# Opening the last feed-forward with weights already in SBUF, idle products in its layer norm, paired loads of the Wq and Wk tails, and a new product order

## The chip, the cores and the metric

One core of one Trainium2 chip runs the whole program. The metric is device time of one execution in microseconds (us), the median of several executions. TensorE (PE in the profile) multiplies matrices, VectorE (DVE), ScalarE (ACT) and GpSimd (POOL) do the element-wise work, SyncE (SP) issues most DMA transfers.

## The reference

Two layers, each a memory-augmented attention and a gated feed-forward with residuals. The attention walks over 64 segments of 32 tokens; eight memory rows go from each segment to the next, so it is a chain in time.

```python
x = A_x                                                # (1, 2048, 576)
for _ in range(2):
    x = x + _A_ref(_layernorm(x), mem0, Wq, Wk, Wv, Wo, 32)   # 32 heads of 128, 8 memory rows
    x = x + _B_ref(_layernorm(x), w1, w3, w2)                  # silu(x w1) * (x w3), then w2; 4608 wide

def _A_ref(x, mem0, Wq, Wk, Wv, Wo, seg_len):          # cut
    mem = mem0
    for s in range(n_seg):
        h = concat([mem, x[segment s]])                # 8 + 32 rows
        q, k, v = h @ Wq, h @ Wk, h @ Wv
        o = softmax(mask(q k^T / sqrt(128))) v @ Wo
        mem = o[:8]; outs.append(o[8:])
```

## The kernel before

Wq, Wk, Wv and Wo live in SBUF for the whole run. The feed-forward weights do not fit and are streamed, two ring slots at a time, for each job of 128 tokens. Both layers run interleaved, the second seven segments behind. A planner written in Python fixes the order of TensorE's work: one letter for each group of products (Q and q are the projections with 128-row and with 64-row contraction, S scores, T transposes, P probabilities times V, O and o the output projection, F, f and W the feed-forward, p the attention transposes, n the layer norm's transposes before a feed-forward).

```python
FIRST = ("maQQqQQqSq...")      # start up to the steady state, 813 groups
FOUR = ("QQqqQpQqqSVV...")     # four segments, 224 groups
LAST = ("QQpqqQQSqqVv...")     # the end, 654 groups
ORDER = FIRST + FOUR * 11 + LAST
```

The loads at the start: four full pieces of 128 rows and a tail of 64 rows for each of Wq and Wk. The tail of Wq goes to partitions 0 to 63, that of Wk to 64 to 127.

```python
def load_qk(self, kind):
    def f(n):
        wd = (self.a.wq, self.a.wk)[kind]
        for c in range(4):
            self.dma(self.T.W[:, 4 * kind + c, :], wd[c * P:(c + 1) * P, :])
        self.dma(self.T.W[kind * R64:(kind + 1) * R64, 8, :], wd[4 * P:D, :])
    return f
```

The last feed-forward has no attention beside it. Its nine weight blocks (two of the 18 column pairs each) are fetched over the attention weights once these have been read for the last time: blocks 0 to 2 over Wv, 3 to 7 over Wq and Wk, block 8 over Wo.

```python
if last:
    v_done, qk_done, o_done = last_reads
    tail = []
    for i in range(9):
        ...                                   # block 2 in two parts
        tail.append([load("tail", ..., em.tail_load(i, what), deps=dep) ...])
for pp in range(NPR // 2):                    # blocks in order 0 to 8
    for pr_ in (2 * pp, 2 * pp + 1):
        if last:
            w13 = w2 = None
            ld = tail[pp]
        else:
            w13, w2 = Slot("w13"), Slot("w2", users=ne)     # ring slots
            ...
```

## Time and profile before

| | before |
|---|---|
| time | 2783.58 us median, three runs, 2782.71 to 2785.88 |
| span of the profiled execution | 2782.7 us |
| TensorE busy / weight loads busy | 2725.4 / 2245.9 us (98% / 81%) |
| VectorE / ScalarE / GpSimd busy | 2041.0 / 1093.0 / 328.4 us |
| DMA | 323.80 MB, mean 116 GB/s |
| mean granted TensorE clock | 0.993 |

The prediction shows the lines that matter. Two ways of reading are needed for them. In a window, TensorE's busy time near the window's length means that only less work on TensorE, or work at a higher clock, would help there. In a timeline, the bracket at a line's end is TensorE's idle time before that line and what ended it; "issue" stands there when no semaphore explains the idleness.

### The profile page before, as it was taken

How to read it: one execution, taken by the hardware profiler on the slowest of the kernel's cores; microseconds unless marked ns; L12 is line 12 of the kernel's file. 1: busy time of each engine (PE TensorE's matmuls, PEld its weight loads, DVE VectorE, ACT ScalarE, POOL GpSimd, SP SyncE). 2: the span in 40 equal slices, each digit the busy share in tenths (PEclk: the TensorE clock that was granted, in tenths of full speed). 3: DMA queues.
4: the chain of work that ended last, by engine and by line, in shares of the span. 5: the costliest groups of instructions: out<-in, count | busy, mean ns of one | idle time of the engine just before them, and what ended most of it. 6: DMA issues, size and time to landing. Idle time of an engine off the chain costs nothing.

```text
span 2782.7 us, 136378 instructions
## 1 busy us (share of the span) xinstructions
PE 2725.4 (98%) x60909; PEld 2245.9 (81%) x60909; DVE 2041.0 (73%) x5559; ACT 1093.0 (39%) x3364; POOL 328.4 (12%) x399
## 2 busy tenths in 40 slices
PE   5999999999999999999999999999999999999998
PEld 3888878888888888888888888888888888888886
DVE  4677777777777777777777777777777777677765
ACT  1434443433434344343434434343443434343332
POOL 1111010110101011010101101010110101011110
PEclk9999999999999999999999999999999999999998
DMA  8072614234241423424142342414244241423468
GB/s 307 4 207 67 178 56 139 82 111 132 74 139 49 147 82 112 131 75 137 52 145 82 114 130 74 139 52 143 82 116 128 77 139 56 132 84 114 143 180 244
DMA packets 483436, 323.80 MB, mean 116 GB/s; under 512 B 26296, under 2 KB 478400, under 8 KB 481184
## 3 DMA queue, kind: packets, MB, share of 16 engines
q1 hardware_dynamic: 479824, 308.15, 37.5%
q8 instruction: 476, 7.80, 1.1%
q0 software_dynamic: 3024, 6.93, 0.8%
q14 instruction: 112, 0.92, 0.1%
HBM read 310.26 MB, written 2.36 MB: 112 GB/s over the span
## 4 chain that ended last, share of the span: by engine, by line
PE 96%; DMA 1%; DVE 1%; issue 1%; ACT 1%; POOL 0%; SPq 0%; DVEq 0%; ACTq 0%; POOLq 0%
PE bank L538 83%; PE YB L538 13%; DMA W<-in_A_Wk_dram 1%; DMA WO<-in_B_w_dram 0%; DVE STAT L544 0%; ACT OT L541 0%; DVE PB L544 0%; DMA W<-in_A_Wq_dram 0%; DVE SME L544 0%; ACT HT L541 0%; ACT SME L541 0%; DVE XR L544 0%; ACT PTS L541 0%; DVE PTS L544 0%; ACT QKT L541 0%
## 5 line engine op out<-in xcount | busy, mean ns | idle before, releaser
L538 PEld LDWEIGHTS <-W 128*128 128x128 bf16 (+1 forms) x29040 | 1228.7, 98 | 147.9 <-issue 44.2
L538 PE MATMUL bank<-HT,W 128*128 128x80 bf16 (+3 forms) x22720 | 817.7, 198 | 20.6 <-DMA W<-in_A_Wk_dram 12.6
L538 PE MATMUL bank<-XTB,W 128*128 128x256 bf16 (+3 forms) x6320 | 657.5, 262 | 0.3 <-DMA W<-in_B_w_dram 0.3
L895 POOL MEMSET PB<- 128x1024 bf16 x284 | 270.2, 951 | 2134.4 <-PE bank L538 1529.1
L541 ACT ACTIVATE QKT<-bank 128x64 bf16<-128x64 f32 (+1 forms) x1382 | 320.2, 314 | 448.6 <-PE bank L538 441.2
L538 PE MATMUL YB<-OT,WO 128*128 128x80 bf16 (+3 forms) x11360 | 431.5, 199 | 4.8 <-ACT OT L541 3.9
L538 PEld LDWEIGHTS <-WO 128*128 128x128 bf16 (+1 forms) x11400 | 388.5, 102 | 44.6 <-issue 26.9
L538 PE MATMUL bank<-WV,HT 128*32 128x512 bf16 (+1 forms) x6840 | 381.1, 383 | 0.8 <-issue 0.8
L544 DVE CAST QKT<-bank 128x256 bf16<-128x256 f32 (+2 forms) x682 | 184.1, 317 | 186.9 <-PE bank L538 185.5
L538 PE MATMUL bank<-W2C,HTT 128*128 128x288 bf16 x2232 | 312.9, 287 | 0.0
L544 DVE TENSOR_REDUCE STAT<-SME 104x8 f32<-104x320 f32 (+1 forms) x568 | 270.9, 477 | 56.4 <-ACT SME L541 53.5
L538 PEld LDWEIGHTS <-HT 128*32 128x32 bf16 (+1 forms) x6840 | 150.3, 95 | 180.0 <-issue 56.3
L544 DVE TENSOR_TENSOR PB<-SME,STAT 40x128 bf16<-40x128 f32 (+1 forms) x1004 | 283.9, 321 | 12.6 <-DVE STAT L544 0.9
L541 ACT ACTIVATE HTT<-bank 128x512 bf16<-128x512 f32 (+1 forms) x324 | 176.4, 550 | 261.8 <-PE bank L538 261.4
L538 PEld LDWEIGHTS <-HTT 128*128 128x128 bf16 x2304 | 209.9, 98 | 54.3 <-issue 1.5
L544 DVE SCALAR_TENSOR_TENSOR XR<-bank,XR 128x288 f32<-128x288 f32 x576 | 239.5, 448 | 12.3 <-PE bank L538 7.4
L541 ACT ACTIVATE SME<-SME 104x320 f32<-104x320 f32 (+1 forms) x284 | 133.5, 470 | 265.7 <-DVE SME L544 265.1
L544 DVE SCALAR_TENSOR_TENSOR HTT<-HTT,bank 128x512 bf16<-128x512 bf16 (+1 forms) x324 | 201.8, 623 | 41.6 <-ACT HTT L541 38.9
L541 ACT ACTIVATE OT<-bank 128x320 bf16<-128x320 f32 (+1 forms) x352 | 138.1, 413 | 214.7 <-PE bank L538 214.6
L544 DVE TENSOR_TENSOR HTT<-HTT,bank 128x512 bf16<-128x512 bf16 (+1 forms) x324 | 203.5, 628 | 22.4
L544 DVE TENSOR_TENSOR SME<-bank,maskb 104x320 f32<-104x320 f32 (+1 forms) x284 | 135.7, 484 | 113.2 <-PE bank L538 106.7
L541 ACT ACTIVATE V<-bank 128x512 bf16<-128x512 f32 x248 | 138.4, 596 | 181.6 <-PE bank L538 181.2
(64 smaller groups left out, 1707.7 us busy)
## 6 DMA issues: line engine op xcount, KB each, us to landing
W<-in_B_w_dram SPq DMA_DIRECT2D x612, 256.0 KB, 3.5
W2C<-in_B_w_dram SPq DMA_DIRECT2D x306, 288.0 KB, 3.2
W<-in_B_w_dram SPq DMA_DIRECT2D x612, 32.0 KB, 3.1
W<-in_B_w_dram SPq DMA_DIRECT2D x10, 512.0 KB, 8.3
WO<-in_A_Wo_dram SPq DMA_DIRECT2D x4, 1152.0 KB, 16.6
XR<-in_A_x_dram POOLq DMA_DIRECT2D x16, 288.0 KB, 3.7
W<-in_A_Wq_dram SPq DMA_DIRECT2D x4, 1024.0 KB, 8.3
W<-in_A_Wk_dram SPq DMA_DIRECT2D x4, 1024.0 KB, 17.3
```

The lines of the kernel that those rows point to most:

```text
L538: self.ch("PE", self.nc.tensor.matmul(out, lhsT=lhsT, rhs=rhs, start=start, stop=stop, skip_group_check=True, **k))
L541: self.ch("ACT", self.nc.scalar.activation(*a, **k))
L544: self.ch("DVE", getattr(self.nc.vector, fn_)(*a, **k))
L895: return lambda n: self.ch("POOL", self.nc.gpsimd.memset(self.T.PB[:, pb.i], 0.0))
```

## The change

It has four parts. The last feed-forward begins with block 8, whose weights its predecessor left in the two ring slots, so eight blocks are fetched. Ten products of the identity with 512 columns of Wo, whose result nobody reads, stand before the transposes of the last layer norm to keep TensorE's clock up. The two 64-row tails are issued one after the other, behind all full rows. And the three order strings are new throughout; in the last one the predecessor's down-projection (W) moves ahead of the layer norm's transposes (n).

```diff
+        npp = NPR // 2
+        for at, pp in enumerate([npp - 1] + list(range(npp - 1)) if last else range(npp)):
+            stays = last and pp == npp - 1
             for pr_ in (2 * pp, 2 * pp + 1):
-                if last:
+                if stays:
+                    w13, w2 = kept[pr_]
+                    ld = []
+                    w2s.append(w2)
+                elif last:
                     w13 = w2 = None
                     ld = tail[pp]
                 else:
-                    w13, w2 = Slot("w13"), Slot("w2", users=ne)
+                    keep = s0 < nst <= s0 + 4 and pp == npp - 1
+                    w13, w2 = Slot("w13", users=1 + keep), Slot("w2", users=ne + keep)
+                    kept[pr_] = w13, w2
 ...
-            for i in range(9):
+            for i in range(8):
 ...
     def f(n):                                   # load_qk
-            self.dma(self.T.W[kind * R64:(kind + 1) * R64, 8, :], wd[4 * P:D, :])
+            if kind:
+                for r, wd in ((0, self.a.wq), (1, self.a.wk)):
+                    self.dma(self.T.W[r * R64:(r + 1) * R64, 8, :], wd[4 * P:D, :])
 ...
     def f(n):                                   # ln_tr
+            for _ in range(10 if warm else 0):
+                self.mm(self.T.YB[:], self.T.ident[:], self.T.WO[:, 0, 0:512], True, True)
             for c in range(5):
                 ...                             # the transposes
 ...
-    "maQQqQQqSq..."   ... "pnWFFffFfFWfFfFW..."  # FIRST, FOUR, LAST rewritten
+    "maQQqqSQQq..."   ... "pWnFFffFfFWfFFffW..."
```

More of the change, by code (lines that the diff above doesn't have):

```diff
@@ L187 @@
 FIRST = (
-    "maQQqQQqSqQqqSQqQQqqSSTVvVPTPvTOoPOToXOPxoOoQQqqQQSqqQqSQqVQqvSTQqPTSOPOToPoTOPoOoaQQqqVSvQQqqQQqqSTVSPvQqQqTOSP"
-    "oXTOPoTOPoOoxQQqqQQSqqQqSQVvqQSTqQqPSOoTPTOPoTOPoOoQQpqqQQqqSVSvQnQqqFTFffVSPvQTQqPqOFfOTFoSoPfWOXxTFfPFOoofWQQq"
-    "qQQSqqFQfqSFWQfqVvSTQqPFTQfPqOSWoFTOPfoFTOfPWOooFQQqqfaQFfqSWQQqFfVvQSqqWTFFffVPvSWQQqqOSTFfPFfToOWoPTPOOoobQQqq"
-    "QQSqqXQxSqQTQqVvqSPQTqOPSXxToOPoTOPoOoQQpqqQQSqqVVSvvQnTQqqQPqSQTFfqFOfPSoTOFoPfXxOTFPfWOooFQfqFQqfQWQSqqVvSQWQq"
-    "qQTFqfSPQTFqfXxSFOofPWOTFfPoTaFfPOOWooFQqfQQqqFQqfVSvWQFqfQFSqWQSfqQTFfqVSvWPFfTFfPOToWPOoTOPobOoXxQpqQQqqXxSQQq"
@@ L193 @@
-    "qVSTvQqPQqSTQqOPSoTOPoOTPonOoQQqqQpQqqSVVvvQTQqSqPQQSqqnOTFfPFoSfXxTFfPOWWFTOofPFOfooWFWQqfQQqqFQqfXxSWWQQqqVSvT"
-    "FQfqFQPfqSTOWWaFoSPfFTOofPWTOPFWOFooffVvWQQqqQqSQWFfqQQTqqSWFfPSQOTWqFfPFQqfVSoWWFTfvOPoTWPOOoobQQpqqVQSqvQQqQqS"
-    "qQSqXTxQqPTSXxPOoTOPoTWPOOoon"
+    "maQQqqSQQqQQqSQqqTqSQVvVqPvTOPSToOPXOToPoxOoQQqqQQSqqQSqVQqvQSTqPQTqPSTOoPOOToPoaOoQQqqQQqqSVSvQQqqQTSqQqPVSTOPv"
+    "oTXPOToPOOooxQQqqQQSqqQqSQQqVSqQqvTSPTOPoTOPoTOPoOoQQpqqVQvqSQnQqqFQqfSTFfPSQQqqWFTOPfSoFOfVvTWFPfoXTFPOOoofxQqQ"
@@ new lines @@
+    "QqqQFSqfVSvQWQqqQTqSQPqFfOTFfPSoTWPOFofOTFPfoOoWQQqqFQfqVvWFQqfSFQSfqVvWQFqfQSqTFfPQOTqWFPfSoTFPfOOWToPoOoabQQqq"
+    "QQqqSVSvQQqqXxTSXxPQTQqqOSPToPOOToPoOoQQpqqQQSqqQQqqSVVvvTnQPqSFTQPfqOFSofXTOoPxWTFFfPfOOooWQQqqFfQFSfqQQqqVSvQT"
+    "QqqFQPfSqFWSfXTFfPxOTOWooPFTFffPOOooWQFqfQqQFafqQWFSqfQQqqSFWQqfVVSvvFfTQqPWFSfTFfPOToWPOoTOPoOboQQqqQpQSqqQXxSQ"
+    "qqVSvQqTQPqXTSPxOTOoPoTPOOoonQQpqqQQSqqVnQqSvQQqqFTfFPfQOTqSoFWVvSfPFTWOPfXTOFxofPFOWooWQfqQQqqQFfqSVvWFWQTqfSQX"
+    "xqFWQqPfSWQTOqPFoSfOTFPfoWFTWOPfFOooWQfqQQqQqqSWQFfqSVvFTQqWQqfWaQqPFSSfTFVvfPOWWFTfoOPoTWPOOoobQQqqQQSqqQQSqqVX"
@@ L196 @@
+    "TvSxQqPQTqOoSPXxTOPopTWPOOoon"
 )
 FOUR = (
-    "QQqqQpQqqSVVvvQTQqPqSnQQSqqOFTFPffoSXxTOWWFPfoTFPfOOFooWQqfQFfqQWQSqqXVxvQTQqqWWFSSfPFQfqOFTQqfFPfoSWWOTFPfoTOFf"
-    "PWOooWQQqqFQqfSWQWQqqFQSfqVvTFWQqPfSWFQfqTOFfPoSWWFVvfTOPoTWPOOooabWQQqqQQSqqQQqqVSSvXxTQqPQqTOPSXxoTOPopTOPoOon"
+    "QQqqQpQSqqVVvvQTQqqPSnQFQSqqfOTFPfSoXxTFfPFWWOFToffPOOooWWFQfqQQqqQFqfSFWWQfqXVxvSQTWQqqFPfSTWQFPfqOOToSoWFPfFTO"
+    "PfWOooFQfqQQqqWWFQqfVSSvQQqqWFTQqfPSWFQfqVvSTWWFFPffOoTOPoTWPOoOoabWQQqqQQSqqQQqqVSSvXxTQqPQqTOPSXxoTOPopTOPoOon"
@@ L200 @@
 )
 LAST = (
-    "QQpqqQQSqqVvnQFfqQSqQTqFPfFTOSPQqfVOWvoSoTFPWOTfXxoPFOfoWFWQqfQQqqFQSqfXVxvWWQTFqfSFQqfQqQqPSFTWOWPfSoTOPFWOToof"
-    "PFOfoWQQqqVvFQfqSWWFQfqFQqfQqSWTFPfQQSqqWTFSPfVvWTWOFfoOPoTWPOoOobQQqqQpQSqqQQqqSXVxSvQqTQPqTXxPSOOoTWPToPOOoonQ"
-    "QpqqVSvQqQQnqqQTFPSqfQQSqqOFTfVvPFToSfPOWOooWTFPfXOWxoWQQqqVSvFQqfQqFQQqqfSTFPfQSqWWOFTQqfFPfoSTWWFOPfoTFPfWWOOF"
-    "oofFQqQfqQqSWQWFqfFfTQQSqqQWqWFQqfSVvFfPSWOWTFfPVovTWPTOoPOOoobWQQQqqqpQSVXqxvQSnQqqFfTQSPqQFqfOFToSfPWTOFPfoTOP"
-    "FOfooWQQqqQFqfSQFqfVSvQQqqQTWFqfPSQTqFOoSfPVvFTOPWTOoofPFOoXfxQWQqqVSvQFfqQFqfQSqWTQFfqQSqQPqFTSOfPoWTOPFTofPOOo"
@@ L207 @@
-    "oFQqQqfQQSqqWQSqVvQTQQqqqSPSTVPvFOOTooPfTOoPOopnWFFffFfFWfFfFWfFfFfWFfFfWFfFWfFfFWfFFffWFfFfWW"
+    "QQqqQpQqqSVvSQnQqqQTqQFqPfSSFTOPfVvFTOoofPFWWTOPfoFOfoWQWFqfQQqqWFWQSfqVXxvQSqXxQqTFQqPfSQFfqOTFWPfoSWOTFfPFTOoo"
+    "fPWOWoFQqfFWWQqfFQSfqQVvqQWQSqqWTFQfqQSPqWFTOSoPfVWFvfTOPoTWPOOoobQqpQQqqQSqQqSXVvxQTqQSPqQTqXPSOxoOTWPToPOOoonQ"
+    "QqqpQSqVQnvqQTSqPFQfqFQTOqfPSFQOqfVoSovWWTFfPFTOPfWOFWooXxQqfVQqvQQSqqWQqSFTQqfFWQQqSqPfTFSPfOWTOooWPFTFfPfOOooW"
+    "WQFfqQqFQQqfqSWFWQqfSVvFQfqWWSFQqfTFfPQqWTWOFSoPfVvTOWoPTWPOObooQQpqqQQSqqQQqqSnXVvxFfSTQqPQFTqfOoSPFTOoPfWTOPFO"
@@ L208 @@
+    "fooFQqfQqVSQvQqqWQTFfqFSPfVQqvWTQFSfqFQPqfOOoSoWTFfPXxTFPfWOOooFQfqQqQQSqqQSVqvWQTFfqQSPqFfQqTOSoPWOTFPfoTFfPOOo"
+    "oWQqFQfqQQSqqVvSQQqqQTQqqSPTSVPFvOToOPoTfOoPOopWnFFffFfFWfFFffWFfWFfFfFWfFfFWfFFffWFfFfWFfFfWW"
 )
@@ L260, in make_nodes, with ln_nodes @@
     steps = [{} for _ in range(nst)]
-    def ln_nodes(tag, src, xn, deps, prio, writes):
+    def ln_nodes(tag, src, xn, deps, prio, writes, warm=False):
         a = node("DVE", 1.16, em.ln_stats(src, xn), deps=deps, prio=prio, acq=[] if src is xn else [xn], name=tag + "stats")
@@ L267, in ln_nodes @@
         b = Slot("bank", users=len(writes))
-        d = node("PE", 5 * 0.056, em.ln_tr(xn, b), deps=[c], prio=prio, mode="full", acq=[b], rel=[xn], name=tag + "tr")
+        d = node("PE", 5 * 0.056, em.ln_tr(xn, b, warm), deps=[c], prio=prio, mode="full", acq=[b], rel=[xn], name=tag + "tr")
         out = []
@@ L385, in step @@
             last_reads[1].extend(me[f"QKt{u}"] for u in range(8))
-            last_reads[2].extend(wots[:2])
         nxt = [li for li in ls if t - LAG * li + 1 < nseg]
@@ L408, in make_nodes @@
     last_up = [None]
-    last_reads = [], [], []
+    last_reads = [], []
+    kept = {}
     def job(j):
@@ L425, in job @@
             pa = post(bi, g)
-            wr += ln_nodes("F", xr[g], Slot("xn"), [pa], s0, [((lambda bi: lambda b: em.xtb_write(bi, b))(bi), cost, [prev_ff])])
+            wr += ln_nodes("F", xr[g], Slot("xn"), [pa], s0, [((lambda bi: lambda b: em.xtb_write(bi, b))(bi), cost, [prev_ff])], last)
         mm = (128 * ne / 2.4 + 2.5) / 1000
@@ L430, in job @@
         if last:
-            v_done, qk_done, o_done = last_reads
+            v_done, qk_done = last_reads
             tail = []
-            for i in range(9):
+            for i in range(8):
                 if i == 2:
@@ L436, in job @@
                 else:
-                    parts = [(None, 9 * 512 + 4 * 576, v_done if i < 2 else qk_done if i < 8 else o_done)]
+                    parts = [(None, 9 * 512 + 4 * 576, v_done if i < 2 else qk_done)]
                 tail.append([load("tail", kb(128, c), s0 + o.tail_at + 0.01 * i, em.tail_load(i, what), deps=dep) for what, c, dep in parts])
-        for pp in range(NPR // 2):
+        npp = NPR // 2
+        for at, pp in enumerate([npp - 1] + list(range(npp - 1)) if last else range(npp)):
             mids, w2s, htts, lds = [], [], [], []
+            stays = last and pp == npp - 1
             for pr_ in (2 * pp, 2 * pp + 1):
-                prio = s0 + o.ff + (o.win if s0 + 4 < nst else o.last_win) * pr_ / NPR
-                if last:
+                prio = s0 + o.ff + (o.win if s0 + 4 < nst else o.last_win) * (2 * at + pr_ % 2) / NPR
+                if stays:
[3 more added lines that the diff above has]
+                elif last:
                     w13 = w2 = None
@@ L453, in job @@
                 rel13 = [w13] if w13 else []
-                fm = node("PE", 16 * mm, em.ffn_up(ents, pr_, w13, b, last, False), deps=wr + ld, prio=prio, mode="full",
+                fm = node("PE", 16 * mm, em.ffn_up(ents, pr_, w13, b, last and not stays, False), deps=wr + ld, prio=prio, mode="full",
                           acq=b + [htt], name="FF")
-                ff = node("PE", 2 * mm, em.ffn_up(ents, pr_, w13, b, last, True), deps=[fm], prio=prio + o.fft, mode="row",
+                ff = node("PE", 2 * mm, em.ffn_up(ents, pr_, w13, b, last and not stays, True), deps=[fm], prio=prio + o.fft, mode="row",
                           rel=rel13, name="FFt")
@@ L464, in job @@
                 b = banks()
-                d = node("PE", 8 * 0.1225, em.ffn_down(bi, pp, htts, w2s, b, last), deps=mids + lds, prio=prio + o.w2,
+                d = node("PE", 8 * 0.1225, em.ffn_down(bi, pp, htts, w2s, b, last and not stays), deps=mids + lds, prio=prio + o.w2,
                          mode="full", acq=b, rel=htts + w2s, name="W2")
@@ L638, in f @@
             T = self.T
-            qk, wv, wo = T.W[:].rearrange("p a b -> p (a b)"), T.WV[:], T.WO[:].rearrange("p a b -> p (a b)")
+            qk, wv = T.W[:].rearrange("p a b -> p (a b)"), T.WV[:]
             n13, n2 = 9 * 512, 4 * D
@@ L645, in f @@
                 t13, t2 = wv[:, 2 * k:2 * k + n13], qk[:, 5 * k:5 * k + n2]
-            elif i < 8:
+            else:
                 t13, t2 = qk[:, (i - 3) * k:(i - 3) * k + n13], qk[:, (i - 3) * k + n13:(i - 2) * k]
-            else:
-                t13, t2 = wo[:, 0:n13], wo[:, n13:k]
             fa = i * 512
@@ L714, in lnps, with ln_tr @@
         return self.bk_bf(b, 5 * P).rearrange("p (c t) -> p c t", c=5)
-    def ln_tr(self, xn, b):
+    def ln_tr(self, xn, b, warm=False):
         def f(n):
+            for _ in range(10 if warm else 0):
+                self.mm(self.T.YB[:], self.T.ident[:], self.T.WO[:, 0, 0:512], True, True)
             for c in range(5):
```

## The prediction

> **What bounds the kernel now.** I read the page first, then the windows (busy time per stretch), then the chain of waits at both ends, then TensorE's timeline. The windows say where time can be had. Columns: stretch, length, then busy microseconds and instruction counts of TensorE, its weight loads, VectorE, ScalarE and GpSimd, then TensorE's granted clock, DMA share, GB/s.
>
> ```profile
> 20.00:40.00 20.00, 10.53 (x328) 9.68 (x329) 5.64 (x16) 2.72 (x9) 0.00 (x0) 1.00 1.01 376
> ...
> 1000.00:1500.00 500.00, 499.23 (x10804) 411.85 (x10797) 376.49 (x1025) 201.35 (x613) 58.63 (x70) 1.00 0.36 105
> ...
> 2720.00:2740.00 20.00, 13.57 (x393) 11.08 (x390) 12.41 (x34) 5.69 (x21) 4.36 (x5) 0.80 0.88 269
> 2740.00:2760.00 20.00, 20.00 (x248) 16.33 (x248) 11.26 (x29) 5.12 (x12) 0.58 (x1) 0.85 1.10 332
> 2760.00:2783.00 23.00, 16.51 (x201) 12.36 (x198) 11.74 (x29) 3.64 (x9) 0.00 (x0) 0.93 0.62 188
> ```
>
> Between about 66 and 2720 us TensorE is full: 499.23 of 500 us in the middle, at full clock, DMA at a third. Nothing but less TensorE time helps there. The first 60 and the last 50 us are different: DMA saturated, TensorE partly idle and partly at half clock. All three named edits are at those ends. The chain that ended last, in order of time (start, length, what):
>
> ```profile
> 1.62 5.19 DMA W<-in_A_Wq_dram
> 6.81 0.02 issue
> 6.83 21.51 DMA W<-in_A_Wk_dram
> 28.34 0.05 issue
> ...
> 2739.88 23.16 PE bank L538 x289
> 2763.04 9.57 DMA WO<-in_B_w_dram
> 2772.61 0.05 issue
> 2772.66 5.90 PE bank L538 x50
> ```
>
> The start waits for Wk until 28.34. The end waits for the ninth weight block, which lands at 2772.61, and then does the last block's products, 5.90 us. The timeline of that end (start, length, work, count, idle before and its releaser):
>
> ```profile
> 2769.32 1.15 PE L538 MATMUL bank<-W,HTT 128*128 128x288 bf16 x8
> 2770.91 0.40 PE L538 MATMUL bank<-XTB,WO 128*128 128x128 bf16 x4 [0.44 <-DMA WO<-in_B_w_dram]
> 2772.66 3.52 PE L538 MATMUL bank<-XTB,WO 128*128 128x128 bf16 x36 [1.35 <-DMA WO<-in_B_w_dram]
> ```
>
> **What the Trainium skill says.** "TensorE: Matmul & The Clock Gate", Part 1: after about 3.4 us of idleness the clock halves, and it returns only after a busy window of that length; windows run free of the kernel. The trace agrees: the 2 us windows show clock 0.50 from 2734 to 2744 and 1.00 from 2746, and again 0.50 in 2774 to 2776 after the DMA wait. "SBUF — State Buffer", Door 1, says a 64-partition transfer reaches half of the DMA ports; agreed: while the Wq tail (64 rows of 8192 bytes, 0.52 MB) was in turn, 14 to 16 us moved 217 GB/s, against 397 just before and 418 from 18 us on. The same page, "Can I just issue two DMAs to hit both halves?", says no: two such DMAs gained 6% over one. If so, loading the tails together saves no transfer time. "Runtime: NRT & Kernel Launch", Instruction fetch mechanics: each sequencer fetches its instructions in 16 KiB blocks by DMA. That fits idle time that the trace puts to "issue" only while DMA is saturated (3.44 us before 43.87, 2.04 us before 2733.22); that the fetch causes it is my inference.
>
> **The change part by part.**
>
> *Last feed-forward.* Before: nine weight blocks of (9 x 512 + 4 x 576) x 128 x 2 bytes = 1.77 MB are fetched, issued from 2722.25, landed at 2772.61: 15.9 MB in 50.4 us, 316 GB/s. After: eight, because block 8 is still in the two ring slots where the previous feed-forward left it. The last weight lands about 1.77 MB / 0.33 MB per us = 5.4 us sooner, near 2767.2. In the changed order as many products follow the last read of Wq/Wk as before, so the transfers start equally early.
>
> TensorE's own need: one block in steady state takes 2756.44 - 2753.01 = 3.43 us on the timeline (40 products of 128 columns, 8 of 288). Nine take 30.9 us. Blocks started at 2742.30, so unhindered they would end at 2773.2; they ended at 2778.5. The missing 5.3 us: DMA waits of 0.26 + 0.44 + 1.35 = 2.05; half clock from 2742.30 to about 2745.8, half of 3.5 = 1.75; half clock for about 3.4 us of the last block, about 1.7. The sum, 5.5, closes the account. With block 8 first, block 7 is last, needed at 2742.3 + 8 x 3.43 = 2769.7 and landed at 2767.2: 2.5 us of margin, so the waits (2.05) and the cold last block (1.7) go. At full clock the last product waits for tanh and two multiplications (0.38 + 0.42 + 0.42, against 0.98 us of other products): 0.5 comes back. Gain: 3.2.
>
> *Idle products.* Ten of 512 columns stand in the order after the attention transposes and the predecessor's last down-projection (8 of 288), before the layer norm's transposes. They can run once the attention output has been read, 2735.7. If the clock is down, as before: transposes 0.5, down-projection 1.9, ten at 512/1.2 GHz = 4.3 (0.43 each is an estimate from that skill page), so they end at 2742.5 unless a full busy window ends sooner; the normalised rows are ready at 2739.88. They then delay the transposes by 1 to 2.6 us. In return the down-projection no longer stands between transposes and feed-forward (it had put the start to 2742.30, where the 0.70 us write of the transposed rows alone would allow about 2741.4), and the feed-forward runs warm: +1.75. Net about 1. If the clock never drops: 0.3 + 1.0 + 2.2 = 3.5, ending by 2739.3, no delay, start 2741.3: gain 1.0 + 1.75 = 2.75. Before, it dropped at 2732.2 after the 2 us issue gap, which the same saturated DMA makes likely again, so I weigh the cold case at 60%: gain 1.7.
>
> *Start.* In 14 to 18 and 26 to 30 us, against 422 GB/s, (205 + 107 + 189 + 156) x 2 us = 1.31 MB were not moved: 3.1 us lost to two half-width tails. Wv's two tails already lie side by side; the same count from 38 to 46 us (312, 252, 317, 390) gives 0.83 MB, 2.0 us. So I expect some 1 us saved in transfers. Wk's full rows also come 2.5 us sooner, but TensorE then only reaches Wv sooner, whose full rows come with the transfers. I keep 1.5.
>
> *Product order.* It is rewritten for the whole program, with the same number of groups of each kind. What it can change is switches of array tiling, and waits. One switch costs 0.1 us:
>
> ```profile
> 1004.74 1.15 PE L538 MATMUL bank<-W2C,HTT 128*128 128x288 bf16 x8
> 1005.82 0.46 PE L538 MATMUL bank<-PTS,V 64*128 64x80 bf16 x16
> ...
> 1009.59 1.14 PE L538 MATMUL bank<-W2C,HTT 128*128 128x288 bf16 x8
> 1010.57 5.25 PE L538 MATMUL bank<-HT,W 128*128 128x80 bf16 x144
> ```
>
> The same eight products take 1.08 us up to a group in another tiling, 0.98 up to one in the same. Counting neighbours in the order strings: first part 515 switches before, 508 after; the part repeated eleven times 114 and 114; last part 383 and 375. That is 15 fewer, 1.5 us. The repeated part carries two thirds of the time and ends in the same 40-odd groups, so I give it 0 with an error of 0.3 us a turn, 3 us in all: a new wait there counts eleven times.
>
> *Sum.* 3.2 + 1.7 + 1.5 + 1.5 = 7.9 us of 2783.58: 2775.7.
>
> **The rivals.**
> *The order decides.* Eleven turns multiply any new wait: 0.5 us a turn costs 5.5 us and the total is 2781; 0.3 us better gives 2772. For it: the order strings differ nearly everywhere. Against: the middle already idles only 0.77 us in 500, so there is little to win, and equal switch counts speak for equal time.
> *Idle products in the way.* If they run cold to the end and the layer norm waits, the feed-forward starts at 2743.9, and its clock gain is eaten: 2777.5. For: granted clock 0.50 through 2734 to 2744. Against: they themselves fill the window.
> *DMA stays the bound.* If saturated transfers run slower or start later, the margin of 2.5 us goes, TensorE waits for block 7 and cools again: about 2779. Against: DMA share stays at 1.10 there, and 1.77 MB less must move.
> *Tails don't overlap.* Then the start gains nothing in transfers and the total is about 2777.
>
> **Range and chances.** The parts are small and mostly independent: errors of about 2 at the end, 1.5 at the start, 3.5 from the order make some 4.5 together. So 2775.7, with 2768.5 to 2782. Two per cent is 56 us, more than the start's and end's idle time that this could remove, and no part can cost that: within 2% is nearly sure.
>
> **What would show it.** Right: no DMA wait of TensorE after the last layer norm, granted clock 1.00 for nearly all of the last feed-forward, about 31 us from its first product to its last; the Wk wait of the chain ends some 2 to 3 us sooner; a turn of the repeated part as long as before (162.2 us from one turn's first product to the next's in the trace), with TensorE over 99.5% busy. Wrong: new idle time before TensorE in the middle, transposes held back past the normalised rows by more than 2.6 us, or a DMA wait of TensorE for the eighth block.

## The result and the profile after

The changed kernel took 2775.48 us median (2774.15 to 2775.73, four runs); the kernel before in the same session 2783.59 us (2782.71 to 2785.88). The ratio is 0.9969, with a 95% interval of 0.9951 to 0.9986. Ratios here are the mean time of one kernel's fast runs over the mean of the other's in the same rounds, so they are not quite the ratio of the medians. The predicted time was 2775.7 us.

Windows of the changed kernel, in the columns that the prediction explains:

```profile
20.00:40.00 20.00, 11.10 (x304) 9.97 (x305) 5.90 (x17) 2.61 (x10) 0.32 (x1) 0.94 1.01 346
1000.00:1500.00 500.00, 499.23 (x10828) 415.20 (x10825) 374.82 (x1023) 201.87 (x611) 58.27 (x70) 1.00 0.36 105
...
2730.00:2750.00 20.00, 18.92 (x228) 14.16 (x228) 11.76 (x31) 4.23 (x10) 1.13 (x2) 0.91 1.10 331
2750.00:2772.00 22.00, 17.55 (x234) 13.60 (x232) 13.47 (x33) 4.41 (x11) 0.00 (x0) 0.99 0.70 210
```

The middle is as full as before, to the last digit: 499.23 of 500 us. The end is fuller and mostly at full clock. The chain that ended last, start and end of it (start, length, what):

```profile
2.02 7.37 DMA W<-in_A_Wq_dram
9.40 20.50 DMA W<-in_A_Wk_dram
...
2754.70 9.08 DMA W<-in_B_w_dram
2763.79 0.05 issue
2763.83 2.32 PE bank L547 x36
```

The wait for Wk did not end sooner: 29.90 against 28.34 us before. It is now the Wk tail that ends it, not the full rows. At the end a transfer still stands in the chain, but it is the eighth block's and it lands at 2763.79, not the ninth's at 2772.61. The timeline of that end shows what the wait is worth:

```profile
2762.67 0.39 PE L547 MATMUL bank<-XTB,W 128*128 128x128 bf16 x4
2763.83 2.28 PE L547 MATMUL bank<-XTB,W 128*128 128x128 bf16 x36 [0.77 <-DMA W<-in_B_w_dram]
2766.04 2.43 PE L547 MATMUL bank<-W,HTT 128*128 128x288 bf16 x16
```

There is one wait of 0.77 us where there were three of 2.05 us together, and the 36 products of the last block take 2.28 us against 3.52 before: they run at full clock.

**Where the time went between the two profiled executions** (spans 2782.7 and 2772.4 us; the changed kernel's profile is of its fastest run, so the whole difference is 10.3 us here and 8.1 us in the medians). The milestones are first products of groups, in each trace; the rows sum to 10.1 us, and the other 0.2 lie after the last product:

| stretch | before | after | difference |
|---|---|---|---|
| start to the first product of the repeated part | 552.95 | 549.88 | -3.1 |
| eleven turns of the repeated part | 1784.11 (162.2 each) | 1784.46 (162.2 each) | +0.4 |
| from there to the first transfer of the last weights | 385.19 | 384.47 | -0.7 |
| from that transfer to the attention's transposes | 13.53 | 11.45 | -2.1 |
| from these to the first product of the last feed-forward | 6.52 | 6.34 | -0.2 |
| from that to the last product | 36.25 | 31.87 | -4.4 |

The largest part is the last feed-forward, as predicted. Two entries need an explanation: 3.1 us at the start though all of Wk came no sooner, and 2.1 us before the attention's transposes, where the change did nothing. The second is an idle time put to issue that the kernel before has and this execution has not. It is the last of these lines of the kernel before's timeline:

```profile
2730.92 0.27 PE L538 MATMUL bank<-PTS,V 64*128 64x40 bf16 x7
2733.22 0.21 PE L538 MATMUL bank<-PTS,V 64*128 64x40 bf16 x1 [2.04 <-issue]
```

These are eight products of one group, with the same semaphores behind them, and 2.04 us between the seventh and the eighth.

### The profile page after: what moved, and what is told of

It is laid out like the page before. It is cut to its first block, busy times and chain, and to the rows that moved or that the text cites. A ratio compares the mean times of both kernels' runs of the same rounds, so it can differ in the third digit from the quotient of the medians.

```text
span 2772.4 us, 136269 instructions
## 1 busy us (share of the span) xinstructions
PE 2723.5 (98%) x60919; PEld 2252.7 (81%) x60919; DVE 2047.1 (74%) x5584; ACT 1091.0 (39%) x3339; POOL 328.4 (12%) x399
## 3 DMA queue, kind: packets, MB, share of 16 engines
HBM read 308.49 MB, written 2.36 MB: 112 GB/s over the span
## 4 chain that ended last, share of the span: by engine, by line
PE 96%; DMA 2%; ACT 1%; DVE 1%; issue 0%; SPq 0%; ACTq 0%; DVEq 0%
PE bank L547 82%; PE YB L547 14%; DMA W<-in_A_Wk_dram 1%; DMA W<-in_B_w_dram 1%; DMA WV<-in_B_w_dram 0%; SPq L556 0%; DMA W<-in_A_Wq_dram 0%; ACT OT L550 0%; DVE STAT L553 0%; ACT HT L550 0%; DVE SME L553 0%; ACT PTS L550 0%; DVE PB L553 0%; DVE PTS L553 0%; ACT QKT L550 0%
## 5 line engine op out<-in xcount | busy, mean ns | idle before, releaser
L547 PE MATMUL bank<-XTB,W 128*128 128x256 bf16 (+1 forms) x6360 | 658.2, 261 | 1.6 <-ACT XTB L550 0.8
L550 ACT ACTIVATE QKT<-bank 128x64 bf16<-128x64 f32 (+1 forms) x1348 | 312.6, 315 | 445.0 <-PE bank L547 434.4
L553 DVE CAST QKT<-bank 128x64 bf16<-128x64 f32 (+1 forms) x716 | 193.6, 316 | 243.5 <-PE bank L547 242.3
L550 ACT ACTIVATE PTS<-bank 128x320 bf16<-128x320 f32 (+1 forms) x386 | 146.5, 411 | 206.1 <-PE bank L547 143.0
L550 ACT ACTIVATE V<-bank 128x512 bf16<-128x512 f32 x269 | 147.2, 596 | 173.9 <-PE bank L547 173.4
```

What stands on the lines that cost most here:

```text
L547: self.ch("PE", self.nc.tensor.matmul(out, lhsT=lhsT, rhs=rhs, start=start, stop=stop, skip_group_check=True, **k))
L550: self.ch("ACT", self.nc.scalar.activation(*a, **k))
L553: self.ch("DVE", getattr(self.nc.vector, fn_)(*a, **k))
```

## The experiments

The theory to be tested, P: the parts of the prediction add up; the kept block is the largest, the idle products come next, the order gives little. The main rival, O: the order decides, and the named edits matter little. Rivals on single parts: I, the idle products are in the way; S, pairing the tails saves no transfer time. Twelve runs were made, one of them the changed kernel itself once more; all gave correct results. "Ratio" is to the kernel before of the same session.

| run | edit, against the changed kernel unless said | median us | ratio and 95% interval |
|---|---|---|---|
| after_again | none | 2775.59 | 0.9969 [0.9957, 0.9981] |
| order_alone | kernel before with the new strings | 2780.68 | 0.9992 [0.998, 1.0004] |
| old_order | old strings | 2777.61 | 0.9978 [0.9966, 0.999] |
| no_idle | no idle products | 2775.82 | 0.9975 [0.9963, 0.9987] |
| nine_blocks | weights not kept | 2780.27 | 0.9988 [0.9975, 1.0] |
| tails_apart | Wq tail in its old place | 2776.21 | 0.9972 [0.9958, 0.9986] |
| idle_5 | 5 idle products | 2774.39 | 0.9965 [0.9953, 0.9978] |
| idle_20 | 20 idle products | 2777.62 | 0.9977 [0.9964, 0.9989] |
| tails_two_queues | tails first, on two queues | 2773.46 | 0.997 [0.9957, 0.9982] |
| tails_pieces | tails in alternating pieces | 2774.75 | 0.9971 [0.9956, 0.9986] |
| late_fetch | last weights held back | 2782.82 | one look |
| pieces_idle_5 | tails in pieces, 5 idle products | 2771.86 | 0.9963 [0.9949, 0.9976] |

The intervals are about 0.12% wide to each side, 3.4 us. So times tell the large parts apart and traces the small ones. The cleanest measure of the end is the stretch from the attention's transposes to the last product, because neither the start nor the issue gap lies in it. Each row is one trace, and its sum also holds what the clock did in that execution:

| | transposes to first feed-forward product | first to last feed-forward product | sum |
|---|---|---|---|
| before | 6.52 | 36.25 | 42.77 |
| order_alone | 5.60 | 37.06 | 42.66 |
| nine_blocks | 6.72 | 33.87 | 40.59 |
| old_order | 5.37 | 32.14 | 37.51 |
| no_idle | 5.61 | 32.49 | 38.10 |
| changed kernel, first profile | 6.34 | 31.87 | 38.21 |
| after_again | 6.01 | 30.92 | 36.93 |
| tails_apart | 6.08 | 30.92 | 37.00 |
| idle_5 | 6.09 | 30.93 | 37.02 |
| idle_20 | 9.57 | 30.92 | 40.49 |
| tails_two_queues | 6.04 | 30.93 | 36.97 |
| tails_pieces | 7.07 | 30.93 | 38.00 |
| pieces_idle_5 | 6.09 | 30.93 | 37.02 |

### The changed kernel once more

> The changed kernel unaltered, a second profile and five rounds. Both theories: 2775.5 within 1 us, 8 us below the kernel before. What it is for: whether the end of the attention again runs without the 2 us gap that the kernel before had there (if the gap is an accident of instruction fetch and not of the order, it comes and goes), and whether TensorE again waits about 0.8 us for the second piece of block 7.

The time repeats: 2775.59 us. The gap is back, at another product and in another group:

```profile
2729.25 0.35 PE L547 MATMUL YB<-OT,WO 128*128 128x40 bf16 x8 [0.39 <-ACT OT L550]
2731.48 1.01 PE L547 MATMUL YB<-OT,WO 128*128 128x40 bf16 x32 [1.87 <-issue]
```

With the gap TensorE reaches the feed-forward 1.8 us later against the transfers (19.64 us after the first of them, 17.80 in the first profile), and the wait for block 7 is gone: the feed-forward takes 30.92 us, which is nine blocks of 3.43. That is why one execution with 2 us less before the transposes is not 2 us faster in all. But the gap alone does not decide on the wait. tails_pieces has neither: its clock was at half while the idle products ran, so it too came to the feed-forward late, after 19.04 us. old_order has both, a gap of 1.23 us and a wait of 1.21 us that ends at 2767.17; its profile names a VectorE write, but the second piece of block 7 landed at 2767.12. There the feed-forward began 17.75 us after the first transfer. In the ten traces that load eight blocks early, those two with 17.8 us waited and the eight with 19.0 us or more did not.

### The order alone, and the named edits alone

```diff
 # order_alone: the kernel before
-FIRST, FOUR, LAST = before
+FIRST, FOUR, LAST = after
 # old_order: the changed kernel
-FIRST, FOUR, LAST = after
+FIRST, FOUR, LAST = before
```

> The kernel before with only the new order strings. Theory P (the parts add: order 1.5 to 3, the named edits the rest): 2780 to 2782. Rival O (the order decides): 2775 to 2777. The repeated part should stay at 162.2 us a turn in both.

> The changed kernel with the old order strings, so the three named edits alone. Theory P: 2777 to 2779, that is 5 to 6 us gained. Rival O: 2782 to 2783. In the old order the idle products stand before the predecessor's down-projection, so the feed-forward's start may be held up by 1 to 2 us.

The order alone gives 0.08%, 2.2 us, not clear of zero; the named edits alone 0.22%, 6.1 us. Their sum, 0.30%, is the 0.31% of both. O falls, P stands as far as these two sizes go. In order_alone the repeated part takes 1784.35 us for eleven turns, against 1784.11 with the old strings: nothing gained, nothing lost. What the order does at the end can be read from the table: moving the down-projection ahead of the layer norm's transposes lets the feed-forward start 0.92 us sooner (5.60 against 6.52). But without kept weights this only makes TensorE wait for the ninth block sooner, and the sum stays (42.66 against 42.77). With idle products the new order brings no such gain. In old_order, where the down-projection still stands behind the transposes, these come 4.10 us after the attention's transposes, not later than without idle products, and the feed-forward starts after 5.37 us, sooner than with the new order (6.01 to 6.34). The delay of 1 to 2 us that was expected there did not come. Its sum (37.51) is no shorter only because it waits 1.21 us for block 7.

### Without the kept weights

```diff
-        for at, pp in enumerate([npp - 1] + list(range(npp - 1)) if last else range(npp)):
+        for pp in range(NPR // 2):
 ...
-            for i in range(8):
+            for i in range(9):          # block 8 over Wo again
```

> The changed kernel with the predecessor's weights not kept: nine blocks fetched, in the old block order, with idle products, paired tails and the new product order. If the kept block is worth what the prediction says (3.2 us, of which 2.05 waits and 1.7 cold last block, less 0.5): 2778 to 2780, with two DMA waits of TensorE for block 8 of about 2 us together and the clock at half in the last block. The idle products then gain nothing, since they only make TensorE wait longer for block 8: 2780 to 2781. Rival (order and clock luck gave the 8 us): 2776.

The time is 2780.27 us, as expected. The last feed-forward takes 33.87 us against 30.92 in after_again, so the kept block is worth 2.95 us there. In the medians it is 4.7 us. Of the difference, 0.71 us is a later start of the feed-forward in this trace (6.72 against 6.01), whose idle products ran at half clock; the rest lies within the intervals. The timeline names the waits:

```profile
2766.62 2.28 PE L538 MATMUL bank<-XTB,W 128*128 128x128 bf16 x36 [1.00 <-DMA W<-in_B_w_dram]
...
2770.24 0.40 PE L538 MATMUL bank<-XTB,WO 128*128 128x128 bf16 x4 [0.26 <-DMA WO<-in_B_w_dram]
2772.00 2.28 PE L538 MATMUL bank<-XTB,WO 128*128 128x128 bf16 x36 [1.36 <-DMA WO<-in_B_w_dram]
```

The waits are 1.00 + 0.26 + 1.36 = 2.62 us, a little more than in the kernel before. One expectation failed: the last 36 products took 2.28 us, so this time the clock did not fall after the waits. The stretches at half clock in these traces last 3.41 us or multiples of it, so one can count back in steps of that length. Where the clock fell (the kernel before and order_alone), the last such window before the fall held all of the 1.8 us of waiting. In nine_blocks the waits spread over three windows, with 1.0 us at most in one. So the fall after the waits depends on how they lie in the windows and is not a fixed price; three traces suggest this and do not prove it.

### Fewer, no and more idle products

```diff
-            for _ in range(10 if warm else 0):
+            for _ in range(0):                      # no_idle
+            for _ in range(5 if warm else 0):       # idle_5
+            for _ in range(20 if warm else 0):      # idle_20
```

> The changed kernel without its ten idle products. Theory P: the transposes come about 1 us sooner, but TensorE's clock is at half for 3.4 to 6.8 us of the feed-forward, 1.7 to 3.4 us lost; part of that is slack against block 7, so 0.5 to 1.5 us slower than the changed kernel, 2776 to 2777. Rival I (the idle products are in the way, or DMA alone sets the end): 2775.5 or less.

> Five idle products in place of ten. Two traces of the changed kernel have the transposes 0.7 to 1.0 us later after the attention's transposes than the kernel without idle products (5.1 and 4.8 against 4.1 us). If five are enough to keep the clock, the transposes come at 4.1 to 4.4 us and the feed-forward still runs at full clock: 0.5 us faster, 2775. If they are too few, the clock falls or stays down into the feed-forward as without any: 2776 to 2777.

> Twenty idle products, twice the suspected cost. Each of the second ten is on the path if the first ten already reach past the layer norm: 10 x 0.216 = 2.2 us at full clock, so the feed-forward starts 2.2 us later after the attention's transposes (8.2 us against 6.0 to 6.3) and the total is 2777.7. If the idle products had slack, less.

Without idle products, the layer norm's transposes, the first 40 products and the next 36:

```profile
2734.94 0.71 PE L547 MATMUL bank<-ident,XN 128*128 128x128 bf16 x5 [1.46 <-DVE XN L553]
2736.45 3.84 PE L547 MATMUL bank<-XTB,W 128*128 128x128 bf16 x40 [0.79 <-ACT XTB L550]
2740.22 2.28 PE L547 MATMUL bank<-XTB,WV 128*128 128x128 bf16 x36
```

With ten of them (after_again):

```profile
2736.14 2.11 PE L547 MATMUL YB<-WO,ident 128*128 128x512 bf16 x9 [0.19 <-issue]
2738.08 0.44 PE L547 MATMUL bank<-ident,XN 128*128 128x128 bf16 x5
2739.32 2.28 PE L547 MATMUL bank<-XTB,W 128*128 128x128 bf16 x40 [0.79 <-ACT XTB L550]
```

The first 40 products take 3.84 us without and 2.28 us with idle products: 1.56 us were lost to the half clock. The price is that the transposes have no gap before them any more: they come 4.77 us after the attention's transposes, against 4.10 without. The sums give 38.10 - 36.93 = 1.17 us for ten idle products. That is the good case. With ten idle products three traces have 36.93 to 37.00. But tails_pieces, whose clock was down for two windows so that the idle products delayed the transposes by 1.73 us, has 38.00, and the first profile with its wait 38.21, as much as without idle products. The times agree in sign (0.9975 against 0.9969) but their intervals overlap. So rival I falls by the traces, with a gain of 0 to 1.2 us from execution to execution; the times alone do not tell.

Five do as well as ten: the sum is 37.02 in both traces with five (idle_5 and pieces_idle_5), although the clock was down for two windows in both, and the time 0.9965. Twenty cost 3.56 us in the sum, more than the 2.2 expected: in that execution the clock was at half for two windows instead of one, so that part of the twenty ran at half speed. Against tails_pieces, with ten and two such windows, they cost 2.49 us. The time moved by about 2 us (2777.62), within the intervals. So beyond what fills the gap, each idle product was paid in full here.

### The tails

```diff
 # tails_apart
-            if kind:
-                for r, wd in ((0, self.a.wq), (1, self.a.wk)):
-                    self.dma(self.T.W[r * R64:(r + 1) * R64, 8, :], wd[4 * P:D, :])
+            self.dma(self.T.W[kind * R64:(kind + 1) * R64, 8, :], wd[4 * P:D, :])
 # tails_pieces
+            if kind:
+                for s in range(0, H * E, 1024):
+                    for r, wd in ((0, self.a.wq), (1, self.a.wk)):
+                        self.dma(self.T.W[r * R64:(r + 1) * R64, 8, s:s + 1024], wd[4 * P:D, s:s + 1024])
 # tails_two_queues, ahead of all full rows
+            if not kind:
+                self.dma(self.T.W[0:R64, 8, :], self.a.wq[4 * P:D, :])
+                self.ch("ACT", self.nc.scalar.dma_start(out=self.T.W[R64:P, 8, :], in_=self.a.wk[4 * P:D, :]))
```

> The changed kernel with the Wq tail back in its old place, ahead of Wk. Traces so far show the two tails landing one after the other, 2.3 and 2.5 us apart, paired or not. So theory S (the pairing saves no transfer, it only lets the full Wk rows come 3.3 us sooner): Wv's last full rows land at 42.2 us as before and the total is within 1 us of the changed kernel, 2775 to 2776.5. Rival (pairing saves transfer time): 1.5 us or more slower, 2777 or more.

> The changed kernel with both tails at the very start, the Wq tail from SyncE's queue and the Wk tail from ScalarE's, so that one transfer to partitions 0 to 63 and one to 64 to 127 are in flight together. If the two halves can run side by side, both tails are in after about 2.5 us of transfer instead of 5, Wk's last full rows land about 27.4 us and Wv's at 39.5 to 40, and the total may fall by 1 to 2 us. If they serialize (the skill page's 6%), Wk's last full rows land at about 29.9 and Wv's at 42.2, and the total stays within 1 us of 2775.5.

> The changed kernel with each tail cut into four pieces of 1024 columns, taken in turn Wq, Wk, Wq, Wk on the one queue. If finer alternation overlaps the halves, the tails land within 2.5 to 3.5 us after Wk's last full rows instead of 4.9, and Wv's last full rows before 41. If they serialize, 5 us and 42.2, or later for the smaller pieces; total then 2775 to 2776.5.

The times at which transfers had landed, from the traces' records of their completion:

| us | Wk full rows | both tails, all of Wq and Wk | Wv full rows |
|---|---|---|---|
| before | 28.34 | 30.48 | 42.23 |
| tails_apart | 28.16 | 30.21 | 42.21 |
| changed kernel | 25.04 | 29.91 | 42.19 |
| tails_two_queues | 27.91 | 27.91 | 40.95 |
| tails_pieces | 24.43 | 28.33 | 40.87 |
| pieces_idle_5 | 25.46 | 29.81 | 41.87 |

Paired on one queue, the tails land 2.34 and 2.53 us after one another: they take turns, and nothing is saved by the time of Wv. The pairing only changes what TensorE waits for. In the changed kernel:

```profile
25.08 2.08 PE L547 MATMUL bank<-HT,W 128*128 128x40 bf16 x57 [3.01 <-DMA W<-in_A_Wk_dram]
27.43 0.21 PE L547 MATMUL bank<-HT,W 64*128 64x40 bf16 x1 [0.26 <-DMA W<-in_A_Wq_dram]
29.95 0.45 PE L547 MATMUL bank<-HT,W 64*128 64x40 bf16 x15 [2.31 <-DMA W<-in_A_Wk_dram]
```

Full rows are used 3.3 us sooner, then TensorE waits 2.31 us for the Wk tail. The first products with Wv start at 43.55 us in the changed kernel and at 43.55 in tails_apart, both just after a gap put to issue that ends at 43.38 and 43.34. The times (0.9969 and 0.9972) can't be told apart. S stands.

On two queues the halves take turns as well: the tails land at 6.02 and 8.22 us, 2.20 us after one another, and from 4 to 8 us DMA moves 238 GB/s, hardly more than with whole tails on one queue (217 from 24 to 28 us). All of Wq and Wk is in 2.0 us sooner all the same. This edit also moved the tails to the very start, where the first of them is issued at 0.74 us, before any other weight (1.62 in the changed kernel), and DMA moves 294 GB/s from 2 to 4 us instead of 202. How much of the gain is place and how much the queue was not tested. The pieces do overlap in part: 281 GB/s from 24 to 28 us, and 3.90 and 4.35 us from Wk's full rows to the last tail in two traces, against 4.87. All of Wq and Wk is in 1.6 us sooner in one trace, but only 0.1 us in the other, which started later.

On two queues TensorE gains nothing from it: a gap put to issue ends at 43.40 us, and Wv is first used at 43.61. With pieces Wv is first used at 39.17 and 40.75 us, and the repeated part begins at 545.3 and 546.9 us, sooner than in all other traces (547.9 or later). The times do not resolve it. The ratios of 0.997 and 0.9971 are those of the changed kernel, the first with four runs of 2772.83 to 2774.27 us and one of 2781.39.

### The gap before the attention's end

In the traces I counted TensorE's instructions (weight loads, products, waits) up to each idle time of over 0.7 us that is put to issue, in the start's and the end's saturated DMA. Wherever there is such a gap, it stands at one of the same counts: 449, 705, 1217, 1473 and 121025. All of these leave 193 on division by 256, and the kernels have different work at these places. Counted over the whole of all 14 traces, after the first 20 us, there are 49 such gaps, and all 49 leave 193. A transfer of 16384 bytes on the instruction queue ends some 1.5 us before TensorE goes on (1.2 to 1.6 at the end in the eleven traces with a gap). In the kernel before, that transfer starts 3.2 us after TensorE has passed the boundary before it (2.4 to 4.7 us in the eleven traces). So what TensorE lacks is the next block of its own instructions. To test that, the weights' transfers were held back behind the attention's last read of one tile:

```diff
-            last_reads[1].extend(me[f"QKt{u}"] for u in range(8))
+            last_reads[0].append(wots[3])
+            last_reads[1].extend([*(me[f"QKt{u}"] for u in range(8)), wots[3]])
 ...
+            if not self.tail_w:
+                self.dma(T.PTS[:, 0, 0:D], self.a.x[0:P, :])   # waits for the last read of PTS; never read
```

> The changed kernel with one small transfer set before the last feed-forward's weights that must wait for the last read of the attention weights' tile, so that the weights start about 9 us later. The fetch of TensorE's instructions then meets idle DMA rings. If the 2 us gap near the attention's end comes from that fetch, it is gone (no idle time put to issue from 2715 to the last layer norm). The price is known: 45 us of transfers from about 2728 end near 2773, so TensorE waits for the weights again and the total is 2782 to 2786. If the gap stays at 1.5 to 3 us, my cause is wrong.

The waits of TensorE by releaser (total us, times, longest) near the end, kernel before and then late_fetch:

```profile
PE bank L538 <- issue: 2.0, 1, 2.0
```

```profile
PE bank L548 <- DMA W<-in_B_w_dram: 6.9, 9, 1.4
PE bank L548 <- DMA WV<-in_B_w_dram: 1.1, 1, 1.1
...
PE YB L548 <- issue: 0.2, 1, 0.2
```

With idle DMA rings (share 0.01 from 2720 to 2726 us) the gap is gone. The instruction block's transfer started 0.4 us after the boundary before it and had landed at 2724.1, 3 us before its need. The price came as worked out: 8.0 us of waits for the late weights. One execution without a gap would prove little, since two with saturated transfers have none either. But in those two the block landed only 1.5 and 1.3 us before its need, just in time, after a start 2.0 and 2.3 us behind the boundary. So the cause is shown by this run and the landings together: the saturated transfers hold back the instruction fetch. Whether a given execution pays nothing or up to 2.9 us for it varies: of the thirteen traces with early weights (the kernel before among them), the first of the changed kernel and that of tails_pieces have no gap there, the other eleven 1.2 to 2.9 us.

### A version that may be better than both

> The changed kernel with the tails in four alternating pieces and five idle products, the two variants that looked no worse put together. In the traces the pieces bring Wv's last full rows 1.3 us sooner, and five idle products cost nothing against ten. If both reach the end: 2773 to 2774.5, ratio to the kernel before 0.9963 or so. If the start's gain is lost to the clock's phase as in the medians so far: 2774.5 to 2776, not to be told from the changed kernel.

2771.86 us median in five runs (2770.87 to 2775.34), ratio 0.9963. It is faster than the kernel before beyond doubt. Against the changed kernel (0.9969) the intervals overlap widely, so it is the best central value and no more than that.

## Why the prediction was right

**The kept block** was put at 3.2 us and measured 2.95 (nine_blocks against after_again). The account behind it held in its terms: 45.0 us from first transfer to the last needed piece (2763.79 - 2718.81) against the predicted 2767.2 - 2722.25 = 44.95, and nine blocks at 3.43 us. Terms were off and partly cancelled. The cold last block (1.7 us) is not a constant: nine_blocks waited, for 2.62 us instead of 2.05, and stayed warm. The 0.5 us that was to come back at the last product did not show: 30.92 us is nine times 3.43 with 0.05 left.

**The margin** of 2.5 us for block 7 was about 1 us too large. The prediction took the block's need to come 8 x 3.43 = 27.4 us after the first product, but the block's first products run before the previous block's down-projection, and its second piece is needed after 26.46 us (in both traces of the changed kernel). So on its own times the margin was 1.5 us; after_again had 1.9. In the first profile the gap was absent, 2.25 us went with it (first transfer to first feed-forward product 17.80 us instead of 20.05), and 0.77 us of waiting appeared. The prediction named a DMA wait for the eighth block as a sign of being wrong, and by that sign this step was wrong in the first profile, though for 0.77 us only.

**The idle products** were put at 1.7 us, from a delay of 0 to 2.6, an earlier start of 0.9 and 1.75 us of clock. Measured: a delay of 0.7 to 1.7 in the five traces with ten products, the new order and eight blocks loaded early, an earlier start of 0.92 (which belongs to the order string that moves the down-projection, as order_alone shows, and which old_order has without it once the clock is up), 1.56 us of clock; net, 1.17 in the good case and about nothing in two other traces. On the clock the prediction says that the trace agrees with a fall after about 3.4 us of idleness. It agrees on the length of the windows, not on that: in the kernel before the clock fell at 2732.18 us, after a window in which products ran for 2.36 of 3.41 us. The two traces of the changed kernel fell on each side of the two cases: in one the clock was down when the idle products began and rose during them, in the other it rose just as they began.

**The start** was put at 1.5 us, 1 us of it saved in transfers. That step failed: paired tails save nothing, and its sign, a wait for Wk that ends 2 to 3 us sooner, did not come (29.91 against 28.34). What misled me, it seems, was the comparison with Wv's two tails, which lie in rows of 2048 bytes and alternate more finely; tails_pieces, with rows of 2048 bytes, does gain some. The skill page that I quoted against it was right for whole tails. The start's 3.1 us in the first profile has another origin. Traces with the new order and paired whole tails reach the repeated part at 548.6 to 552.6 us, and the half-clock time in their first 200 us runs from 3.4 to 17.1 us. The kernel before had 20.5 us of it and the changed kernel's first profile 17.1, and a stretch at half clock can cost up to half its length. A part of this is chance of the clock's windows; tails_apart (551.76) lies within it. How much of the start's gain is order, pairing or chance is left open.

**The order** was put at 1.5 us for 15 switches less, with the repeated part at 0 within 3 us. The repeated part moved by 0.2 to 0.4 us in 1784, as expected. The order alone gave 2.2 us within 3.4, which fits 1.5 and does not prove it. In the last part before the transfers, where eight switches should have given 0.8 us, one trace shows 0.7 less, the others with the new order between 1.6 less and 1.0 more.

So the sum was right to 0.2 us while single terms were off by up to 1.5 us. It was right because the two large terms, kept block and idle products, came from a closed account of the last feed-forward, and because the errors of the others had both signs. The second is luck, and so is a hit within 0.2 us: the start's saving in transfers did not exist, and the order's 2.2 us are known only to within 3.4.

## What to carry to other kernels

At the end of a program that is otherwise bound by TensorE, write down the last stage as an account: pure work at full clock, each wait, each stretch at half clock. When it closes to a few tenths, each part of a change can be priced from it. Work that is inserted to hold the clock should just fill the gap that is there: here every product beyond that was paid. And when a gap carries no semaphore and DMA is saturated, count instructions before looking for a cause in the order: here all such gaps stood 256 instructions apart or multiples of it.

## What the Trainium skill lacked or had wrong

- "SBUF — State Buffer", "Can I just issue two DMAs to hit both halves?": it says that they serialize, 6% over one. Two whole 64-row tails agree, on one queue (2.34 and 2.53 us after one another) and on two (2.20 us apart). Cut into alternating pieces with 2048-byte rows they overlapped in part: 281 GB/s from 24 to 28 us against 217, and 3.90 and 4.35 us for both tails against 4.87.
- "Runtime: NRT & Kernel Launch", Instruction fetch mechanics: it calls the cost of crossing a block mostly hidden. Its 256 instructions a block agree with the traces. It lacks that a saturated DMA uncovers the fetch: TensorE stood for 0.7 to 3.4 us at such a boundary in the start and up to 2.9 us at the end, and not at all at the one boundary where the rings were idle (late_fetch).
- "TensorE: Matmul & The Clock Gate", Part 1: it does not say how full a busy window must be, and the share of products in the profile does not tell it either. In after_again a window from 2732.7 to 2736.1 with products for 78% of it brought the clock back; one with 74% (the kernel before, 2739.0 to 2742.4) left it at half, and so did one with 98% (idle_20, 37.16 to 40.57). Nor did the clock fall only after idle windows: it fell at 2732.18 in the kernel before after a window with products for 69%.
- "TensorEngine Tiling (Array Packing)", Key Properties: it says that a change of tiling mode drains TensorE, without a cost. Here it cost 0.1 us (in the kernel before eight products took 1.08 us up to a group in another tiling, 0.98 up to one in the same).
